# A gated recurrence followed by a maxout layer: the weights are requested through another engine's queue, the filling products are spread differently, and the written order of the whole program is replaced

## The chip, the cores and the metric

The program runs on one NeuronCore of one Trainium2 chip. The metric is device time in microseconds (us) of one execution. The kernel before takes 151.06 us, the median of 3 runs (150.87 to 151.34). A profiled execution has a span of its own: the time from its first to its last instruction.

In the text TensorE is PE (its weight loads PEld), VectorE is DVE, ScalarE is ACT, GpSimd is POOL and SyncE is SP. SP and ACT can both request transfers from memory (DMAs); each has a queue of its own.

## The reference, cut to what matters

```
def _attn_ref(q, k, v, alpha):            # 4 batches, 8 heads, 768 steps, 48 wide, float32
    state = zeros((B, H, D, D))
    for t in range(S):
        state = alpha[:, :, t, :, None] * state + einsum('bhd,bhe->bhde', k[:, :, t], v[:, :, t])
        y[:, :, t] = einsum('bhd,bhde->bhe', q[:, :, t], state)

def _moe_ref(x, w1, w2, w3, w_out):       # x: 3072 x 384 (y with its heads side by side)
    h = maximum(maximum(x @ w1, x @ w2), x @ w3)      # w1, w2, w3: 384 x 768
    return h @ w_out                                  # w_out: 768 x 384
```

## The kernel before, in words

The work is cut into 24 units: unit u is batch u % 4 and the chunk u // 4 of 128 time steps, with all 8 heads. Units 2n and 2n+1 share the loads number n of alpha, q, k and v (tiles `an`, `qn`, `kn`, `vn`). The loads 0 to 3 are asked for in halves, one unit each (192 KB in runs of 192 bytes: 8 heads by 48 floats). A load is named by the letter, n, and 0 or 8 for the first or second unit of the pair: "v 0 0" is v of unit 0, "q 1 8" is q of unit 3.

For each unit there is a chain of named steps. `ln` (ACT) takes the logarithm of alpha; `cums` (PE) sums it along time with a triangular matrix; `ep` and `en` (ACT) are its exponentials; `q~` and `k~` (DVE or POOL) scale q and k; `v` (ACT or POOL) scales v. `turn` (PE) transposes q~ and k~, `qkT` (DVE or ACT) copies them out of PSUM, `scores` (PE) multiplies them, `LA` (DVE) masks them, `outs` (PE) makes y, `xb` (ACT or DVE) casts it, `x turn` (PE) and `xT` (DVE or ACT) turn it into the layout of the layer. The state that is handed to the next chunk goes through `totals`, `e`, `G`, `sums`, `U` and `Z`.

The layer is computed from differences: max(x w1, x w2, x w3) = x w1 + max(0, x (w2 - w1), x (w3 - w1)). `grow` (PE, line 642) multiplies xT by one of the two differences, `relu` (ACT) and `max` (DVE) take the maximum, and `shrink` (PE, line 678) multiplies by w_out. What is left of x w1 is folded ahead: x (w1 w_out), made once by `w1 turn`, `w1T` and `fold` (line 383) and copied by `w1o`. In the names, "grow 1 0 0" is unit 1, the first half of the columns (the last but one digit 0), w2 - w1 (the last digit 0; 1 is w3 - w1).

All weights come in as float32, each matrix in two parts: "weights g p" (line 327) with g = 0 for w1, 1 for w2, 2 for w3, 3 for w_out; part 0 is the first 256 of 768 columns (384 KB), part 1 the other 512 (768 KB). Their tiles are `ws0` to `ws3`. `cast 0 p` (ACT, line 333) makes w1 half precision, `sub g p` (DVE or POOL, line 341) makes w2 - w1 and w3 - w1 (tile `wd`), and `cast 3 p` casts w_out. The first half of the columns of a `grow` needs both parts of `sub`; the second half needs part 1 alone.

The order of everything is written out by hand. The function builds a list of steps (`plan.step`), each with its engines to choose from. `ORDER` is the sequence of all steps over all engines, `PICK` chooses another engine than the first for some steps, `BANKS` gives each product its PSUM bank. `Plan.issue` runs down `ORDER`; every engine then executes its own steps strictly in that sequence. Loads, weights, cross transposes and stores begin in the order of the plan.

A DMA waits, on the engine that requests it, for the landing of the DMA eight places before it in the order of the plan, since they share eight semaphores. All steps that stand behind it on that engine wait along.

`zeros` are products of a cleared tile with itself (`Z1_0`, line 586), whose result nobody reads. They stand in PE's sequence between its early steps: 27 of them, the first behind `k~ 1`'s landing in its tile (`WARM = (1, 1, 27)`: unit, side, number).

Of the kernel before, what the change touches and what calls it, by code (L numbers as in the profile page):

```python
# [15 lines left out]

CDEC = 0.92
SIG = 128.0

NBANKS = 8  # L20
LEAD = (2.0, 4.0, 6.5, 5.0)
WCUTS = (0, 256, 768)
HALF_LOADS = 4
WARM = (1, 1, 27)
SINGLE, LAST = 4, 2
PAIRS = 10
CASTING = ()
# [5 lines left out]


ORDER = (
# [44 lines left out]
)  # L80
BANKS = (
# [9 lines left out]
)  # L91
PICK = {
# [8 lines left out]
}  # L101


TRANSFERS = ("load", "weights", "cross", "store")
BEHIND = mybir.DependencyInfo(mybir.DependencyClass.NoSync, mybir.DependencyReason.DATA)
HARD, HARD_LOAD, HARD_LATE, LATE_FROM = 0.5, 1.8, 1.5, 3


# [4 lines left out]
def weight_options(share, cast):  # L113
    if cast:
        return [("POOL", 0.6 + 0.4 * share, 0, 3.7 * share, 0.2)]
    return [("SP", HARD, 0, 3.25 * share + 0.1, 0.6)]


def cross_options(work):
# [55 lines left out]
def kernel(  # L175
# [12 lines left out]
    nc = tc.nc  # L188
# [85 lines left out]
        return at  # L274

    hq, ht = rotate(QKS, MORE[0]), rotate(QKTS, MORE[1])
    for t in las:
        nc.vector.memset(t[:, :, D:], 0.0)
    for t in qks[:QKS]:
        nc.vector.memset(t[:, :, :, D:], 0.0)  # L280
    for zz in Zs:
        for t in zz:
            nc.vector.memset(t, 0.0)

    plan = Plan()
    place, live = {}, {}
# [291 lines left out]
                      out=xT, in_=live[xk]),  # L578
                  reads=[xk], writes=[("xT", cb % NX, b)])

    def warm(u, w, count):
        zero = Zs[1][0].rearrange("p a b -> p (a b)")

        def zeros(e):
            live["wm"] = bank(("wm", 0), [P, DM], FP32)
            nc.tensor.matmul(live["wm"], zero[:, :P], zero, start=True, stop=True)  # L586

        for i in range(count):
            plan.step(f"zeros {i}", [("PE", 0.163)], 90.0, zeros,
                      banks=[("wm", 0)] if i == 0 else [],  # L590
                      reads=([("qk", hq[u], w)] if u >= 0 else []) if i == 0 else [("wm", 0)],
                      writes=[("wm", 0)] if i in (0, count - 1) else [])

    def state(u):
# [122 lines left out]
    for n in range(NG):  # L717
# [6 lines left out]
        for u in range(n * UB, (n + 1) * UB):  # L724
            prep(u)
            if u >= PAIRS and u % UB == 0:
                continue
            if u == WARM[0]:
                warm(*WARM)
            for v_ in (u - 1, u) if u >= PAIRS else (u,):  # L730
                output(v_)
        while due and due[0][-1] // UB + 4 <= n:
# [37 lines left out]
```

## Time and profile before

| | before |
|---|---|
| time, median of 3 | 151.06 us |
| the profiled execution's own time | 150.59 us |
| its span | 148.8 us |
| PE busy | 133.9 us (90%) |
| DVE busy | 106.9 us (72%) |
| ACT busy | 90.5 us (61%) |
| POOL busy | 52.5 us (35%) |
| mean granted PE clock | 0.977 |
| moved by DMA | 31.07 MB, mean 209 GB/s |

Two things help in reading it. PE's share is an average: PE has idle stretches in the first 26 us and none that matter behind them. And the 1.8 us between the span and the execution's own time lie outside the instructions.

### The profile page before, as it was taken

The page shows a single profiled execution, that of the slowest core. Times are in us where ns is not written, and L with a number is a line of the kernel's source. Part 1 is how long each engine was busy: PE and PEld are TensorE (multiplying, and loading weights), DVE is VectorE, ACT ScalarE, POOL GpSimd, SP SyncE. Part 2 cuts the span into 40 slices and gives each one's busy share as a digit, 9 for nine tenths or more (in the row PEclk, how much of TensorE's full clock was granted, in tenths as well). Part 3 has the DMA queues.
Part 4 walks back from the last instruction along what each step waited for, and adds up shares of the span by engine and source line. Part 5 has one row for each costly group of instructions (what it writes and reads, how often), then busy time and mean ns, then how long its engine had stood idle before and what let it go on. Part 6 is the DMA issues. An engine that isn't in the chain of part 4 may idle for free.

```text
span 148.8 us, 4162 instructions
## 1 busy us (share of the span) xinstructions
PE 133.9 (90%) x1683; PEld 104.6 (70%) x1683; DVE 106.9 (72%) x186; ACT 90.5 (61%) x184; POOL 52.5 (35%) x75
## 2 busy tenths in 40 slices
PE   0575297999999999999999999999999999999991
PEld 0233266968787886888787797787878877689781
DVE  7239318487998898979697779998578878584140
ACT  3531976948667587797746686745475844554331
POOL 0050041202523414840597709448029290170000
PEclk9999659999999999999999999999999999999999
DMA  5999999999999999999999999899998999704322
GB/s 115 205 225 322 202 341 269 283 267 173 223 208 219 237 220 210 248 184 250 266 266 263 185 197 250 163 215 269 177 232 160 243 325 189 147 4 131 109 82 79
DMA packets 116131, 31.07 MB, mean 209 GB/s; under 512 B 109712, under 2 KB 114960, under 8 KB 116112
## 3 DMA queue, kind: packets, MB, share of 16 engines
q1 hardware_dynamic: 83888, 21.17, 69.7%
q10 hardware_dynamic: 32224, 9.64, 28.7%
q8 instruction: 13, 0.21, 0.6%
q14 instruction: 6, 0.05, 0.1%
HBM read 23.69 MB, written 4.72 MB: 191 GB/s over the span
## 4 chain that ended last, share of the span: by engine, by line
PE 85%; SPq 5%; DMA 4%; ACT 2%; DVE 2%; issue 0%; ACTq 0%
PE psum L642 33%; PE psum L678 24%; PE psum L499 5%; PE psum L483 4%; SPq L308 4%; DMA vn<-in_v_dram 4%; PE psum L545 3%; PE psum L572 3%; PE psum L442 3%; PE psum L542 2%; PE psum L604 2%; PE psum L383 2%; PE psum L586 2%; PE psum L412 1%; DVE wd L341 1%; ACT w1h L333 1%
## 5 line engine op out<-in xcount | busy, mean ns | idle before, releaser
L642 PE MATMUL psum<-xT,wd 128*128 128x256 f16 (+1 forms) x540 | 54.4, 251 | 0.9 <-DVE wd L341 0.9
L642 PEld LDWEIGHTS <-wd 128*128 128x128 f16 x540 | 42.9, 98 | 6.9 <-DVE wd L341 1.7
L658 DVE TENSOR_TENSOR hT<-psum,hT 128x512 f16<-128x512 f32 (+1 forms) x39 | 24.3, 644 | 10.3 <-PE psum L642 4.7
L504 DVE TENSOR_TENSOR LA<-psum,c 128x1024 f16<-128x1024 f32 x24 | 28.6, 1219 | 3.1 <-PE psum L499 2.5
L653 ACT ACTIVATE hT<-psum 128x512 f16<-128x512 f32 (+1 forms) x39 | 21.5, 570 | 14.6 <-PE psum L642 13.6
L678 PE MATMUL psum<-wo,hT 128*128 128x384 f16 (+1 forms) x150 | 27.7, 320 | 0.0
L617 POOL TENSOR_TENSOR Z<-U,G 48x192 f16<-48x192 f32 x29 | 16.4, 572 | 12.5 <-DVE U L611 11.4
L678 PEld LDWEIGHTS <-hT 128*128 128x128 f16 x150 | 14.5, 98 | 8.9
L454 POOL TENSOR_TENSOR qk<-qn,ep 128x384 f16<-128x384 f32 x11 | 10.9, 998 | 15.1 <-ACT ep L447 13.3
L678 PE MATMUL psum<-w1o,xT 128*128 128x384 f16 (+1 forms) x75 | 15.8, 319 | 0.0
L450 ACT ACTIVATE en<-psum 128x384 f32<-128x384 f32 x24 | 11.9, 495 | 4.3 <-PE psum L442 3.8
L402 ACT ACTIVATE la<-an 128x384 f16<-128x384 f32 (+1 forms) x16 | 10.8, 689 | 5.7 <-DMA an<-in_alpha_dram 5.7
L454 POOL TENSOR_TENSOR qk<-kn,en 128x384 f16<-128x384 f32 x8 | 8.3, 1042 | 16.6 <-ACT en L450 12.7
L556 ACT ACTIVATE xb<-psum,c 128x384 f16<-128x384 f32 x16 | 9.1, 582 | 8.0 <-PE psum L545 5.8
L447 ACT ACTIVATE ep<-psum 128x384 f32<-128x384 f32 x24 | 11.7, 496 | 2.6 <-DVE qk L454 0.9
L693 ACT COPY ob<-psum 128x384 f32<-128x384 f32 (+1 forms) x18 | 8.3, 468 | 7.8 <-PE psum L678 5.1
L442 PE MATMUL psum<-la,c 128*128 128x384 f16 x24 | 7.8, 347 | 5.6 <-ACT la L402 5.5
L461 ACT ACTIVATE v<-vn,c 128x384 f16<-128x384 f32 x14 | 8.3, 614 | 6.2 <-DMA vn<-in_v_dram 6.2
L545 PE MATMUL psum<-v,LA 128*128 128x48 f16 x192 | 11.1, 186 | 0.0
L611 DVE TENSOR_TENSOR U<-psum,Z 128x384 f32<-128x384 f32 x16 | 8.5, 551 | 3.1 <-PE psum L604 2.5
L545 PEld LDWEIGHTS <-LA 128*128 128x128 f16 x192 | 9.8, 98 | 0.6 <-issue 0.2
L464 POOL TENSOR_SCALAR v<-vn,c 128x384 f16<-128x384 f32 x10 | 6.3, 635 | 9.4 <-DMA vn<-in_v_dram 9.0
(61 smaller groups left out, 189.6 us busy)
## 6 DMA issues: line engine op xcount, KB each, us to landing
out_dram<-ob ACTq DMA_DIRECT2D x20, 192.0 KB, 3.3
an<-in_alpha_dram SPq DMA_DIRECT2D x7, 384.0 KB, 6.6
ws<-in_moe_w_dram SPq DMA_DIRECT2D x3, 768.0 KB, 6.1
kn<-in_k_dram SPq DMA_DIRECT2D x5, 384.0 KB, 6.5
vn<-in_v_dram ACTq DMA_DIRECT2D x5, 384.0 KB, 6.6
an<-in_alpha_dram SPq DMA_DIRECT2D x8, 192.0 KB, 4.0
kn<-in_k_dram SPq DMA_DIRECT2D x8, 192.0 KB, 4.4
qn<-in_q_dram ACTq DMA_DIRECT2D x4, 384.0 KB, 5.3
```

The costliest lines, as they stand in the source:

```text
L402: lambda e, lo=lo * H, hi=hi * H: nc.scalar.activation(out=la[:, lo:hi, :D], in_=an[:, lo:hi, :], func=AFT.Ln, scale=1.0 / CDEC),
L442: nc.tensor.matmul(live[Lk], tri, la[:, hs, :D], start=True, stop=True)
L447: lambda e: nc.scalar.activation(out=ep, in_=live[Lk], func=AFT.Exp),
L450: lambda e: nc.scalar.activation(out=en, in_=live[Lk], func=AFT.Exp, scale=-1.0),
L454: lambda e, w=w, x=x, d=d: engines[e].tensor_mul(qk[:, w, :, :D], ld[x][n % LOADED][:, hs], d),
L504: lambda e: nc.vector.tensor_mul(LA.rearrange("p a b t -> p (a b) t"), live[Ak].rearrange("p a (b t) -> p (a b) t", t=P), maskA.unsqueeze( ...
L545: nc.tensor.matmul(yp[:, 2 * j + p, :], LA[:, p, j, :], v16[:, 2 * j + p, :], start=(cb == 0), stop=True, skip_group_check=True)
L617: lambda e, rows=rows, cols=cols: engines[e].tensor_mul(Zn[rows, :, cols], (Us[u % 3] if cb else live[pk])[rows, :, cols], G[rows, i * NP: ...
L642: nc.tensor.matmul(live[gk][:, jj, :], wd[:, kt, g, j * P:(j + 1) * P], xT[:, kt, :], start=(kt == 0), stop=(kt == NFT - 1))
L653: lambda e, h=h, gk=gk: nc.scalar.activation(out=h, in_=live[gk], func=AFT.Relu),
L658: lambda e, h=h, gk=gk: nc.vector.tensor_max(h, live[gk], h),
L678: nc.tensor.matmul(live[ok][:, cols], a[:, i * P:(i + 1) * P], w[:, cols], start=(kt == 0), stop=(kt == nk - 1))
```

## The change

Four edits go together.

1. A weight request may now go through ACT (a second choice in `weight_options`), and the new `PICK` takes it for all eight (among its first rows: 32, 34, 36 to 40 and 42). None is left on SP.
2. The zero products: 46 instead of 27, without the dependence on `k~ 1`. The tile that they multiply is cleared first of all on DVE.
3. `ORDER`, `BANKS` and `PICK` are new from the first to the last row. The numbers of the steps shift by the 19 added zeros.
4. With it some steps change engines: `sub 1 1` and `sub 2 0` go from DVE to POOL; `qkT` moves towards ACT (7 instead of 4), `ob` towards DVE (12 instead of 7), stores towards SP (10 instead of 4), loads towards ACT (21 instead of 15).

```
-WARM = (1, 1, 27)
+WARM = 46
 ORDER = (
-    4, 8, 9, 5, 6, 0, 10, 12, 34, 7, 32, 1, 11, 2, 123, 65, 127, 82, 84, 128, 129, 83, 64, 131,
...
+    6, 4, 0, 10, 8, 20, 5, 1, 9, 3, 2, 32, 64, 65, 34, 142, 78, 68, 121, 92, 146, 120, 66, 80,
...
-    return [("SP", HARD, 0, 3.25 * share + 0.1, 0.6)]
+    return [("SP", HARD, 0, 3.25 * share + 0.1, 0.6), ("ACT", 0.45, 0, 3.25 * share)]
...
+    nc.vector.memset(Zs[1][0], 0.0)
     for t in las:
         nc.vector.memset(t[:, :, D:], 0.0)
     for t in qks[:QKS]:
         nc.vector.memset(t[:, :, :, D:], 0.0)
-    for zz in Zs:
-        for t in zz:
-            nc.vector.memset(t, 0.0)
+    for t in Zs[0] + Zs[1][1:]:
+        nc.vector.memset(t, 0.0)
...
-    def warm(u, w, count):
+    def warm(count):
...
-                      reads=([("qk", hq[u], w)] if u >= 0 else []) if i == 0 else [("wm", 0)],
+                      reads=[("wm", 0)] if i else [],
...
-            if u == WARM[0]:
-                warm(*WARM)
+            if u == 0:
+                warm(WARM)
```

Three places show what the new tables do. The first is the start of SP's sequence before: loads (`an`, `kn`, `qn`, `vn`) and weights (`ws0` is w1, `ws1` is w2) stand in one line.

```order
L308 DMA an1_67<-in_alpha_dram 128x8x48
L327 DMA ws0_150<-in_moe_w1_dram 128x3x512
L308 DMA vn0_78<-in_v_dram 128x8x48
L327 DMA ws0_150<-in_moe_w1_dram 128x3x256
L308 DMA kn0_74<-in_k_dram 128x8x48
L308 DMA vn1_79<-in_v_dram 128x8x48
L308 DMA qn0_70<-in_q_dram 128x8x48
L327 DMA ws1_151<-in_moe_w2_dram 128x3x256
L327 DMA ws1_151<-in_moe_w2_dram 128x3x512
```

Now the weights stand in ACT's sequence, here from the cast of w1 on (line 335) to the request of w3's larger part (`ws2`). Between them are `ep` (449), `v` (463), the copies `w1T` (374), `qkT` (492) and `xb` (558).

```order
L335 CAST w1h_148<-ws0_150 128x3x512
L449 ACTIVATE ep0_85<-psum_177 128x384
L335 CAST w1h_148<-ws0_150 128x3x256
L463 ACTIVATE v0_100<-vn0_78,c32_62 128x384
L329 DMA ws1_151<-in_moe_w2_dram 128x3x512
L374 COPY w1T_149<-psum_177 128x768
L463 ACTIVATE v1_101<-vn0_78,c32_62 128x384
L329 DMA ws1_151<-in_moe_w2_dram 128x3x256
L492 COPY qkT2_109<-psum_177 128x1024
L329 DMA ws3_153<-in_moe_w_out_dram 128x2x384
L374 COPY w1T_149<-psum_177 128x768
L558 ACTIVATE xb1_116<-psum_177,c32_62 128x384
```

What moved: a weight is no longer behind other transfers in SP's line, but behind whatever ACT has to do ahead of it. The two parts of w1 are requested earlier in the same sequence, around the first `ln` steps.

The second place is the difference w2 - w1 (`wd` from `ws1` and `w1h`) that the first `grow` needs. Its larger part stood in DVE's sequence before, behind an `LA` (504) and an `xT` (577):

```order
L558 TENSOR_SCALAR xb2_117<-psum_177,c32_62 128x384
L504 TENSOR_TENSOR LA0_112<-psum_177,c16_61 128x1024
L577 COPY xT0_120<-psum_177 128x3x128
L341 TENSOR_TENSOR wd_154<-ws1_151,w1h_148 128x3x512
L577 COPY xT0_120<-psum_177 128x3x128
```

Now both of its parts stand in POOL's, behind the early `q~` and `k~` steps (456) and one `v` (466), and the smaller part of w3 - w1 follows:

```order
L456 TENSOR_TENSOR qk2_93<-kn1_75,en2_90 128x8x48
L456 TENSOR_TENSOR qk2_93<-qn1_71,ep2_87 128x8x48
L456 TENSOR_TENSOR qk0_91<-qn0_70,ep0_85 128x8x48
L466 TENSOR_SCALAR v2_102<-vn1_79,c32_62 128x384
L343 TENSOR_TENSOR wd_154<-ws1_151,w1h_148 128x3x512
L343 TENSOR_TENSOR wd_154<-ws1_151,w1h_148 128x3x256
L343 TENSOR_TENSOR wd_154<-ws2_152,w1h_148 128x3x256
```

What moved: DVE has one such step left (`sub 2 1`), POOL three, in a row.

The third place is the start of PE's sequence. Now one zero product (line 588) stands ahead of the first `cums` (444), which needs the first load of alpha, and two behind it:

```order
L588 LDWEIGHTS Z1_0_137
L588 MATMUL psum_177<-Z1_0_137 128x384
L444 LDWEIGHTS c16_61
L444 MATMUL psum_177<-la0_82,c16_61 128x384
L588 LDWEIGHTS Z1_0_137
L588 MATMUL psum_177<-Z1_0_137 128x384
L588 LDWEIGHTS Z1_0_137
L588 MATMUL psum_177<-Z1_0_137 128x384
```

What moved: before, two `cums` came first and nine zeros behind them. In all, 43 of the 46 zeros now stand ahead of the first `grow` (23 of 27 before), and the last three among the first five.

More of the change, by code (lines that the diff above doesn't have):

```diff
@@ L18 @@
 SIG = 128.0
+TRANSFERS = ("load", "weights", "cross", "store")
+BEHIND = mybir.DependencyInfo(mybir.DependencyClass.NoSync, mybir.DependencyReason.DATA)
 NBANKS = 8
@@ L35 @@
 ORDER = (
[44 rows of a table removed]
[45 rows of a table added]
 )
 BANKS = (
[9 rows of a table removed]
[9 rows of a table added]
 )
 PICK = {
[8 rows of a table removed]
-}
-TRANSFERS = ("load", "weights", "cross", "store")
-BEHIND = mybir.DependencyInfo(mybir.DependencyClass.NoSync, mybir.DependencyReason.DATA)
[9 rows of a table added]
+}
 HARD, HARD_LOAD, HARD_LATE, LATE_FROM = 0.5, 1.8, 1.5, 3
```

122 rows, old and new, of tables (BANKS, ORDER, PICK) are left out of this document.

## The prediction

> **What bounds the kernel now.** I read the slices of the page first (PE at 9 tenths from the eighth slice on), then busy time by stretches of my own choosing, then the chain that ended last. The stretches are cut where the granted clock changes, at the first `grow` (25.69 us) and at the first `shrink` (37.39 us). The columns are length, busy time of PE, PEld, DVE, ACT and POOL with counts, granted clock, DMA share, GB/s.
>
> ```profile
> 9.09:12.50 3.41, 2.41 (x30) 1.43 (x28) 1.19 (x3) 0.23 (x1) 0.99 (x1) 1.00 0.99 279
> 12.50:15.92 3.42, 0.82 (x15) 0.32 (x9) 2.55 (x3) 1.41 (x4) 0.00 (x0) 1.00 1.17 270
> 15.92:19.33 3.41, 1.62 (x12) 1.29 (x13) 1.12 (x2) 3.09 (x5) 0.00 (x0) 0.50 0.87 228
> 19.33:22.75 3.42, 3.42 (x39) 2.26 (x37) 1.09 (x2) 2.55 (x4) 1.64 (x1) 0.50 1.10 352
> 22.75:25.69 2.94, 2.05 (x37) 1.53 (x36) 2.77 (x3) 2.25 (x5) 0.58 (x1) 1.00 1.16 273
> 25.69:37.39 11.70, 11.67 (x170) 9.56 (x171) 7.78 (x10) 8.85 (x19) 2.18 (x3) 1.00 0.96 237
> 37.39:145.78 108.39, 108.36 (x1383) 86.62 (x1381) 85.14 (x143) 67.99 (x142) 45.93 (x65) 1.00 1.02 201
> 145.78:148.80 3.02, 0.00 (x0) 0.00 (x0) 0.36 (x1) 0.00 (x0) 0.00 (x0) 1.00 0.29 98
> ```
>
> From 25.69 to 145.78 us PE is idle for 0.06 us. The rest of the span is a start of 25.7 us, in which PE waits or multiplies zeros, and an end of 3.0 us for the last copy and store. So the program is PE's work plus the time until PE has enough of it. Two stretches of the start run at half the clock (0.50), after a stretch in which PE was busy for 0.82 of 3.42 us.
>
> The chain (start, us, what) says what the start waits for.
>
> ```profile
> 16.29 1.37 ACT w1h L333
> ...
> 17.71 0.82 PE psum L366 x6
> ...
> 23.97 1.68 DVE wd L341
> ...
> 25.69 1.18 PE psum L642 x18
> 26.87 0.16 PE psum L586
> 27.03 0.17 PE psum L572 x3
> ...
> 37.39 1.49 PE psum L678 x9
> ```
>
> w1's larger part is cast at 16.29 us; then PE works on the first three units at half the clock; DVE comes to `sub 1 1` (line 341) at 23.97 us; `grow` (642) begins. A zero product (586) costs 0.16 us at full clock, an `x turn` (572) 0.17.
>
> **The frame of the sum.** Up to `shrink 0 0 0` both orders hold the same 42 steps on PE, zeros aside, and behind it the same steps too, with no zeros. So the span after is (start of the first `shrink`) + 108.4 + 3.0 us, as long as PE is not kept waiting later. I take that wait as zero: the closest hand-overs of the long part stand alike in both orders (`x turn 14`, one copy `xT 14`, then `grow` with 0.55 us of PE work between; `scores 20`, `LA 20`, `outs 20` with 1.46), and PE lost 0.03 us there before. What must be found is when the first `grow` begins, 25.69 us before.
>
> **w1 arrives earlier.** The rows are DMA issues (out<-in, queue, count, size, median us from issue to landing), then requests on SP in order of time.
>
> ```profile
> out_dram<-ob ACTq DMA_DIRECT2D x20, 192.0 KB, 3.3
> ...
> ws<-in_moe_w_dram SPq DMA_DIRECT2D x3, 768.0 KB, 6.1
> ...
> an<-in_alpha_dram SPq DMA_DIRECT2D x8, 192.0 KB, 4.0
> ...
> c<-const ACTq DMA_DIRECT2D x1, 96.5 KB, 2.4
> ```
>
> ```profile
> 0.74 1.07 SPq L308 DMA_DIRECT2D an<-in_alpha_dram  x2
> ...
> 6.70 0.76 SPq L308 DMA_DIRECT2D an<-in_alpha_dram  x1
> 7.51 1.10 SPq L327 DMA_DIRECT2D ws<-in_moe_w_dram  x1
> ...
> 15.34 1.25 SPq L327 DMA_DIRECT2D ws<-in_moe_w_dram  x2
> ```
>
> The eighth load was requested at 6.70 us, so it landed near 10.7 (4.0 later); the first near 4.7: 0.86 us apart. After, SP's first loads are the same kind. w1's smaller part waits on ACT for the fourth of them (it holds that semaphore), 7.3 us; two `ln` of 0.5 us follow, and the larger part goes out at about 8.3 us. Alone it would need 2.4 us (the small constant, nearly all latency) plus its bytes: 768 KB at the 352 GB/s of the best stretch is 2.2 us, so 12.9 us. In a line with loads it took 6.1, so 14.4. A 192 KB store on ACT's queue lands in 3.3 us while loads on SP's take 4.0 and more, so a large request on the second queue is not held up by the first; I take 13.4 us. The page "DMA: Bandwidth & Descriptors" of the Trainium skill (Queues, rings and completion order) says that each DMA engine takes turns between the queues by packet, which would favour 2 KB weight rows over 192-byte load rows; no row here has the two kinds side by side.
>
> **From w1 to the first `grow`.** ACT is the line that everything passes. Before, from the cast to `xb 0`, it was busy for 3.09 + 2.55 + 2.25 = 7.9 us and idle for 1.9 of 9.8. ACT's own rows of before give the prices:
>
> ```profile
> 14.51 0.61 ACT L461 ACTIVATE v<-vn,c 128x384 f16<-128x384 f32 x1 [5.19 <-DMA vn<-in_v_dram]
> 15.03 0.51 ACT L402 ACTIVATE la<-an 128x384 f16<-128x384 f32 x1
> ...
> 41.66 0.48 ACT L693 COPY ob<-psum 128x384 f32<-128x384 f32 x1
> 41.67 0.42 ACTq L308 DMA_DIRECT2D qn<-in_q_dram  x1
> ```
>
> After, the stretch holds one more `v` (0.61) and two `ln` (0.5 each, a little overlapped) for one short `e`: about 9.2 us. The five weight requests in it I cost at nothing: the last two rows show a request that runs beside the copy ahead of it. If that cover is gone (ACT idle and waiting there), each costs 0.42 us, 2.1 in all. With ACT's idle time a little under what it was (1.8 us; PE is warm this time, since the zeros leave it no long gap), `xb 0` ends at 13.4 + 9.2 + 1.8 = 24.4 us, and the first `grow` can begin at 24.6.
>
> It needs `sub 1 1` too.
>
> ```profile
> 20.02 1.64 POOL L341 TENSOR_TENSOR wd<-ws,w1h 128x768 f16<-128x768 f32 x1 [9.30 <-DMA ws<-in_moe_w_dram]
> ...
> 23.89 1.75 DVE L341 TENSOR_TENSOR wd<-ws,w1h 128x1536 f16<-128x1536 f32 x1
> ```
>
> POOL takes 1.64 us for half as many elements as DVE does in 1.75, so `sub 1 1` costs about 3.3 us there instead. w2's larger part is requested when ACT starts `v 0`: a cast (1.37), an `ep` (much like an `ln`) and a cast of half the size are 2.6 us, so 16.0 us, about as before (16.1, the second of the two at 15.34). It lands 4.9 us later (2.4 + 2.2 + some sharing; bounds 4.6 and 6.1), 20.9 us. `sub 1 1` ends at 24.2, `sub 1 0` at 25.8. So the slower engine is hidden: both lines meet at 24.6 us. The third `grow` is the first that needs `sub 1 0`, at 25.6: 0.2 us of waiting.
>
> **The sum.** First `grow` 24.6 instead of 25.69: -1.1. Behind it `x turn 0` is done already (-0.17) and one zero product fewer stands in the way (-0.16). New: 0.2 at the third `grow`, and 0.3 at `scores 3`, whose `qkT 3` moves to ACT behind four `relu` and a `w1o`. Together -0.9 us. `fold` needs w_out, which follows w2 in ACT's queue: the 1.5 MB from w2's smaller part to w_out's larger are 4.4 us at 352 GB/s, so 25.3 us, with some sharing 26, and cast by 28; five `grow`, three zeros and what stands between end at 27.9. Met, without a margin. w3 comes last; its parts are subtracted by 33 us, and the order asks for them at 33 and 34. The 16 zeros that are idle fill in the start cost nothing, as PE waits there anyway; nothing of the 46 stands behind the first `shrink`.
>
> So the first `shrink` begins at 36.5 us, the span is 147.9 us and the execution 149.7 (the span and 1.8 us around it, as in the profiled 150.59). The median of three is 0.5 above the profiled run, so I forecast 150.2 us.
>
> Bounds: w1 at 12.9 and no new waits give -1.9 us; w1 at 14.4 gives +0.1, and uncovered requests add up to 2.1. This case's own range is 149.0 to 150.7.
>
> **Rivals.**
>
> *The loads hold the weights up: slower.* ACT's line is strict. w2's request stands behind `v 0`, which needs the tenth load on SP. At 0.86 us each that is 12.4 us, plus the 3.3 us in which w1 (1.15 MB at 352 GB/s) takes the memory: 15.7, and it is needed at 16.0. In the trace of before ACT stood still for 5.19 us in front of just such a `v`. The third `grow` can begin 4.9 us (landing) and 3 x 1.64 us (POOL) after the request; from a request at 16.9 us on that is 26.7, no earlier than before (25.69 and two `grow` of 0.5), and the gain is gone. If w1 takes its 6.1 us instead of 3.3, the tenth load comes at 18.5 and the `grow` 1.6 us later than before: 152.7 us. For it: a faster w1 means slower loads, for they share one memory path, at a DMA share near 1. Against: only ten loads are asked for. Chance 0.24.
>
> *Nothing is gained: the queues share one service.* Loads asked for before w1 are served before it; w1 lands at 14.5 us and the whole start moves by 1.1 us, onto the old place: 151.3 us. For it: the share of the DMA engines is 0.9 to 1.2 throughout. The same page of the Trainium skill (Issuing engines are not separate DMA queues) speaks for it: requests from several engines interleave on the same 16 DMA engines, and only issue time is saved. By that sentence the whole gain would be gone. Chance 0.14.
>
> *The clock is lost again.* "From the first microsecond" is one zero product; the next follow the first `cums`, after 7 us. A stretch with PE busy for 24% was followed by half the clock, one with 71% was not. From 14.8 us on PE has 24 zeros (3.8 us) and some 4.5 us of products for 9.8 us, 85%, so I expect the clock to hold. If loads leave a gap and it falls for 6.8 us, as before, PE does 3.4 us of that work instead of some 5.8: 2.4 later, of which 1.0 falls into idle time: 151.6. Chance 0.08.
>
> *A wait in the long part.* Every sequence is new; one bank or one load that is late there costs PE directly. 0.5 to 2 us: 150.7 to 152.2. Chance 0.06.
>
> **How the numbers follow.** Forecast 0.48, rivals 0.24, 0.14, 0.08, 0.06. The time is that of the forecast, 150.2. The range 149.0 to 152.6 takes in its lower bound, the case of no gain, the lost clock, the late wait and most of the case with held-up weights. A measurement of this kernel can tell about 0.3% (0.45 us) from no change. Faster by more: nearly all of the forecast and a little of the late wait, 0.49. Within it: the case of no gain and a part of the clock's, 0.16. Slower: 0.35.
>
> **What would show it.** Right: cast of w1 near 13.4 us, first `grow` near 24.6, first `shrink` near 36.5, then PE busy for 108.4 us. Wrong: ACT idle ahead of `v 0` for a DMA for over 1 us; a granted clock of 0.50 anywhere from 15 to 25 us; idle time of PE behind the first `shrink`.

## The result, and the profile after

| | before | after |
|---|---|---|
| time, median of 4 | 151.2 us | 157.0 us (155.56 to 158.31) |
| ratio | | 1.038, 95% interval 1.0315 to 1.0447 |
| profiled execution, its span | 150.59, 148.8 us | 157.59, 155.8 us |
| first `grow`, first `shrink` by the chain | 25.69, 37.39 us | 29.60, 40.70 us |
| from there to the end | 111.4 us | 115.1 us |
| mean granted PE clock | 0.977 | 0.967 |

The change makes the kernel slower by 3.8%; 150.2 us was forecast. Of the 7.0 us of span, 3.3 are lost up to the first `shrink` and 3.7 behind it.

PE's slices of the page after show two holes, each with a fall of the clock beside it (a slice is 3.9 us):

```profile
PE   1095799999999999999499999999999999999992
...
PEclk9999559999999999999969999999999999999999
```

The same stretches as in the prediction, cut at after's own places (length, busy time of PE, PEld, DVE, ACT and POOL with counts, granted clock, DMA share, GB/s):

```profile
9.09:12.50 3.41, 3.41 (x19) 1.72 (x18) 0.00 (x0) 2.02 (x5) 0.65 (x1) 1.00 1.10 340
12.50:15.60 3.10, 1.34 (x8) 0.59 (x6) 0.74 (x2) 0.64 (x1) 0.46 (x2) 1.00 0.83 184
15.60:19.30 3.70, 2.67 (x24) 1.97 (x24) 0.98 (x2) 3.66 (x6) 3.05 (x3) 0.54 1.07 249
19.30:23.10 3.80, 3.80 (x30) 2.55 (x25) 1.22 (x1) 1.01 (x1) 1.71 (x2) 0.55 1.15 313
...
40.70:73.98 33.28, 33.28 (x451) 26.70 (x449) 29.65 (x56) 22.93 (x47) 12.97 (x22) 1.00 1.15 219
73.98:76.27 2.29, 0.04 (x1) 0.01 (x1) 2.29 (x2) 0.52 (x2) 1.81 (x2) 1.00 1.25 245
76.27:82.50 6.23, 6.23 (x52) 3.77 (x53) 3.87 (x6) 2.94 (x6) 2.65 (x4) 0.73 0.85 203
82.50:152.80 70.30, 70.26 (x882) 56.56 (x880) 52.20 (x88) 37.27 (x78) 27.75 (x41) 1.00 0.88 166
```

DVE does nothing at all from 9.09 to 12.50 us; before, units 1 and 2 were scaled by 10.7. PE is then busy at half the clock. In the middle PE stands still for 2.25 us, while DVE is busy without a pause, and the next 6.23 us run at a mean clock of 0.73. That is worth up to another 1.7 us (an estimate, 0.27 x 6.23); what is left of the 3.7 us beside the stop is 1.45. One of the four executions had a granted clock of 1.00 throughout and still took 155.56 us, 2.0 less than the profiled one. By that the clock is some 2 us of the profiled execution's loss, and most of the loss is something else.

The chain that ended last, in the start:

```profile
14.96 1.48 ACT w1h L335
...
19.55 0.76 PE psum L588 x2
...
21.16 1.28 PE psum L588 x4
...
25.38 0.92 PE psum L588 x5
...
29.60 1.51 PE psum L644 x27
...
40.70 1.46 PE psum L680 x9
```

Zero products (line 588) are links of it. The next rows are the loads beside w1 (DMA issues between 6.6 and 8.5 us, with the median time to landing), the spread of the three of k, and the first scaling on DVE that waited for them:

```profile
ws<-in_moe_w_dram ACTq DMA_DIRECT2D x1, 768.0 KB, 7.2
kn<-in_k_dram SPq DMA_DIRECT2D x3, 192.0 KB, 7.9
...
vn<-in_v_dram SPq DMA_DIRECT2D x1, 192.0 KB, 7.7
```

```profile
DMA to landing us min/median/max: 3.5/7.9/8.1
```

```profile
14.86 1.03 DVE L456 TENSOR_TENSOR qk<-kn,en 128x384 f16<-128x384 f32 x2 [10.66 <-DMA kn<-in_k_dram]
```

And before, the two loads of v that were asked for beside w1 in the one queue, and the first scaling on DVE:

```profile
vn<-in_v_dram SPq DMA_DIRECT2D x2, 192.0 KB, 6.0
```

```profile
7.02 0.56 DVE L454 TENSOR_TENSOR qk<-kn,en 128x384 f16<-128x384 f32 x1 [2.81 <-ACT en L450]
```

The first load of k, asked for at 5.9 us, ahead of w1, took 3.5 us; the loads beside w1 take nearly 8. Before, v and k beside w1 took 5.8 to 6.6 us, so loads beside w1 were slow in one queue too, and two queues added 1 to 2 us. The larger part of w1 takes 7.2 us, where it took 6.1; only its smaller part came sooner after its request (5.1 us instead of 6.4). The first `k~` on DVE begins at 14.86 us, 7.02 before. Two things make it late: the new order asks for k of unit 0 as the eighth load (before, two of the first four loads were k), and w1 stands beside it on the other queue.

And ACT's own line in the start:

```profile
21.20 1.01 ACT L492 COPY qkT<-psum 128x1024 f16<-128x1024 f16 x1 [1.94 <-PE psum L485]
...
24.93 0.80 ACT L374 COPY w1T<-psum 128x768 f16<-128x768 f16 x1 [2.72 <-PE psum L368]
24.94 0.38 ACTq L329 DMA_DIRECT2D ws<-in_moe_w_out_dram  x1
```

ACT waits for PE twice, 4.7 us together, and the request of w_out's larger part, which stands behind the second wait, goes out at 24.94 us (17.16 before).

### The profile page after: what moved, and what is told of

It is laid out like the page before. It is cut to its first block, busy times and chain, and to the rows that moved or that the text cites. A ratio compares the mean times of both kernels' runs of the same rounds, so it can differ in the third digit from the quotient of the medians.

```text
span 155.8 us, 4195 instructions
## 1 busy us (share of the span) xinstructions
PE 139.8 (90%) x1702; PEld 107.6 (69%) x1702; DVE 105.3 (68%) x187; ACT 88.2 (57%) x176; POOL 58.1 (37%) x82
## 4 chain that ended last, share of the span: by engine, by line
PE 81%; DMA 7%; DVE 4%; ACT 3%; SPq 1%; issue 1%; ACTq 0%
PE psum L644 29%; PE psum L680 23%; PE psum L501 5%; PE psum L485 5%; DMA ws<-in_moe_w_dram 5%; PE psum L547 3%; PE psum L574 2%; DMA qn<-in_q_dram 2%; PE psum L588 2%; PE psum L544 2%; PE psum L606 2%; DVE ws L456 2%; PE psum L444 2%; SPq L310 1%; PE psum L414 1%; PE psum L385 1%
## 5 line engine op out<-in xcount | busy, mean ns | idle before, releaser
L644 PE MATMUL psum<-xT,wd 128*128 128x256 f16 (+1 forms) x540 | 53.7, 251 | 0.0
L680 PE MATMUL psum<-wo,hT 128*128 128x384 f16 (+1 forms) x150 | 28.5, 328 | 0.0
L619 POOL TENSOR_TENSOR Z<-U,G 48x192 f16<-48x192 f32 x31 | 15.6, 508 | 29.3 <-DVE U L613 24.1
L456 POOL TENSOR_TENSOR qk<-qn,ep 128x384 f16<-128x384 f32 x12 | 11.8, 996 | 12.2 <-ACT ep L449 12.0
L588 PE MATMUL psum<-Z 128*128 128x384 f16 x46 | 13.2, 410 | 1.1 <-DVE Z L279 1.1
L466 POOL TENSOR_SCALAR v<-vn,c 128x384 f16<-128x384 f32 x12 | 7.0, 585 | 14.9 <-DMA vn<-in_v_dram 14.5
L456 DVE TENSOR_TENSOR qk<-kn,en 128x384 f16<-128x384 f32 x8 | 4.7, 598 | 10.7 <-DMA kn<-in_k_dram 10.7
L456 POOL TENSOR_TENSOR qk<-kn,en 128x384 f16<-128x384 f32 x9 | 9.2, 1026 | 6.1 <-ACT en L452 3.3
L588 PEld LDWEIGHTS <-Z 128*128 128x128 f16 x46 | 4.8, 116 | 8.8 <-issue 6.7
L695 ACT COPY ob<-psum 128x384 f32<-128x384 f32 (+1 forms) x13 | 6.1, 467 | 8.1 <-PE psum L680 8.1
```

The lines of the kernel that those rows point to most:

```text
L456: lambda e, w=w, x=x, d=d: engines[e].tensor_mul(qk[:, w, :, :D], ld[x][n % LOADED][:, hs], d),
L619: lambda e, rows=rows, cols=cols: engines[e].tensor_mul(Zn[rows, :, cols], (Us[u % 3] if cb else live[pk])[rows, :, cols], G[rows, i * NP: ...
L644: nc.tensor.matmul(live[gk][:, jj, :], wd[:, kt, g, j * P:(j + 1) * P], xT[:, kt, :], start=(kt == 0), stop=(kt == NFT - 1))
L680: nc.tensor.matmul(live[ok][:, cols], a[:, i * P:(i + 1) * P], w[:, cols], start=(kt == 0), stop=(kt == nk - 1))
```

## The experiments

Ratios are to the kernel before, run beside each experiment on the same chip. "First" times of the experiments are starts in PE's timeline; by it before has its first `grow` at 25.69 and its first `shrink` at 37.25, after at 29.43 and 40.53.

### The stop at 74 us: three scalings on DVE, then one

```
 PICK = {
+    402: 1, 403: 1, 410: 1,        # q~ 12, k~ 12, q~ 13: DVE instead of POOL
```

> The changed kernel with k~ 12, q~ 13 and q~ 12 on DVE instead of POOL, nothing else. Theory (k~ 11 on DVE took 3.56 instead of 0.55 us because POOL worked without a pause beside it): k~ 11 ends by 74 us instead of 76.2, PE's gap of 2.3 us at 74 us is gone, and the half clock behind it as well; the time is 153 to 155. Rival (the load of k that landed at 72.83 us was late): the gap stays at 2 us or more and the time at 156.5 to 157.5.

153.75 us (153.41 to 154.99), ratio 1.0215 (1.0149 to 1.028), against 1.038. The step that PE waited for is `k~ 11`, the first of the two in DVE's row. The timeline of after around it, and the first of the two by itself (min, median and max in ns):

```profile
70.98 1.96 POOL L456 TENSOR_TENSOR ws<-qn,ep 128x384 f16<-128x384 f32 x2
71.46 1.28 DVE L660 TENSOR_TENSOR hT<-psum,hT 128x512 f16<-128x512 f32 x2
...
72.65 4.03 DVE L456 TENSOR_TENSOR ws<-kn,en 128x384 f16<-128x384 f32 x2
72.90 0.99 POOL L456 TENSOR_TENSOR qk<-kn,en 128x384 f16<-128x384 f32 x1
...
73.86 1.93 POOL L456 TENSOR_TENSOR qk<-qn,ep 128x384 f16<-128x384 f32 x2
...
76.27 0.34 PE L485 MATMUL psum<-c,ws 128*128 128x128 f16 x3 [2.25 <-DVE ws L456]
```

```profile
L456 DVE TENSOR_TENSOR ws<-kn,en x1: 3560/3560/3560, 72.7 to 72.7; 128x384 f16<-128x384 f32 x1
```

With the three steps on DVE:

```profile
69.55 1.95 POOL L455 TENSOR_TENSOR ws<-qn,ep 128x384 f16<-128x384 f32 x2
...
71.22 1.16 DVE L455 TENSOR_TENSOR ws<-kn,en 128x384 f16<-128x384 f32 x2
```

```profile
L455 DVE TENSOR_TENSOR ws<-kn,en x1: 693/693/693, 71.2 to 71.2; 128x384 f16<-128x384 f32 x1
```

`k~ 11` took 3.56 us after and 0.69 here. PE's stop is gone, and no half clock follows in the profiled execution. Four other runs below leave these three steps on POOL, and in each of them `k~ 11` takes 3.56 to 3.57 us and PE stands still for 2.2. The load of k that landed at 72.83 us was for POOL's `k~ 12`, not for this.

```
+    402: 1,                        # q~ 12 alone
```

> The changed kernel with q~ 12 alone on DVE; POOL has k~ 12 and q~ 13 left beside k~ 11. If POOL holds DVE off for as long as it works without a pause: k~ 11 lasts 2.5 to 2.7 us (3.56 with three), PE's gap shrinks from 2.3 to 1.2 to 1.5 us. If it is one operation of POOL that holds DVE off, whatever follows: 3.4 to 3.6 still, or 0.9 to 1.4.

```profile
71.95 3.08 DVE L455 TENSOR_TENSOR ws<-kn,en 128x384 f16<-128x384 f32 x2
...
72.20 1.00 POOL L455 TENSOR_TENSOR qk<-kn,en 128x384 f16<-128x384 f32 x1
73.15 0.99 POOL L455 TENSOR_TENSOR qk<-qn,ep 128x384 f16<-128x384 f32 x1
...
74.62 0.56 PE L484 MATMUL psum<-c,ws 128*128 128x128 f16 x7 [1.30 <-DVE ws L455]
```

```profile
L455 DVE TENSOR_TENSOR ws<-kn,en x1: 2614/2614/2614, 72.0 to 72.0; 128x384 f16<-128x384 f32 x1
```

The one execution of it took 155.21 us. `k~ 11` took 2.61 us and PE waited 1.3 us, as the first line expected. In all three runs `k~ 11` ends 0.41 or 0.42 us after POOL's last operation without a pause (75.79, 74.14 and 71.50 us): it does not start before POOL pauses. The page "SBUF — State Buffer" of the Trainium skill (Who interferes with whom, and its Summary: rules for kernel authors) says that a DVE operation with two inputs in SBUF and a GpSimd operation that reads SBUF exclude each other, and that the second to issue waits until the first finishes. The runs agree with the exclusion, but show a wait over as many operations as POOL has in a row. They also agree that one SBUF input does not contend: the two `max` (line 660, one input in PSUM) beside POOL's first two scalings took 0.68 us as elsewhere.

### Queue or order of the loads

```
 PICK = {
-    32: 1, 34: 1, 36: 1, 37: 1, 38: 1, 39: 1, 40: 1, 42: 1,      # after: all eight weights on SP again
```

> The changed kernel with its eight weight requests back on SP's queue, in the same written order. Theory (weights on a queue of their own pass the loads asked for before them, and the three units start late for it): the k load that took 8.1 us takes 3.5 to 5, the first k~ on DVE begins by 11.5 us instead of 14.86, the first shrink at 37.5 to 39 instead of 40.7; the time is 153.5 to 155.5. Rival (the new order of the loads is to blame, not the queue): the first k~ stays behind 14 us, the first shrink at 40 or later, the time 156.5 to 157.5.

159.34 us (157.07 to 160.15), ratio 1.048 (1.039 to 1.058): no faster than with the weights on ACT (1.038, 1.0315 to 1.0447), so neither text was right. In its profiled execution (159.56 us) the k loads take 3.8 to 4.0 us again and the first `k~` begins at 10.27 us, as the theory had it. But w1's larger part, now asked for behind eleven loads at 11.5 us, lands at 16.8. What the loads gain w1 loses. So the new order is slow by itself, without the second queue.

```
-    6, 4, 0, 10, 8, 20, 5, 1, 9, 3, 2, 32,
+    4, 8, 5, 9, 0, 1, 6, 10, 2, 3, 20, 32,      # after, with alpha and k of units 0 to 2 first
```

> The changed kernel with only its first eleven loads in another order: alpha and k of the first three units ahead of q, v and the early alpha of unit 5. The weights stay on ACT. If the order of the loads is to blame: the first k~ begins by 9 us and the first shrink comes at 37.5 or before, the time is 153 to 154. If it is the queue of the weights: k comes early, but q and v of the first units still land at 14.5 us or later, and the first shrink at 39 to 40.7; the time is 155 to 157.

157.08 us, ratio 1.041 (1.036 to 1.046): no gain, and at the upper end of what was expected if the queue is to blame. The first `k~` begins at 9.30 us, but the q loads beside w1 now take 7.2 to 7.7 us and land at 13.6 and 15.0. The first `grow` comes at 26.37 us at a full clock, and then PE waits in the folds for the cast of w_out:

```profile
31.54 1.79 PE L381 MATMUL psum<-wo,w1T 128*128 128x384 f16 x10 [1.48 <-ACT wo L331]
```

So the first `shrink` is at 39.97.

```
-    return [("SP", HARD, 0, 3.25 * share + 0.1, 0.6)]
+    return [("SP", HARD, 0, 3.25 * share + 0.1, 0.6), ("ACT", 0.45, 0, 3.25 * share)]
...
+    32: 1, 34: 1, 36: 1, 37: 1, 38: 1, 39: 1, 40: 1, 42: 1,      # before, all weights on ACT
```

> The kernel before, its order, banks and zeros as they are, with the eight weight requests on ACT's queue. If a second queue for the weights makes the loads late: loads that are under way beside w1 take 6 us and more, the first shrink moves from 37.4 to 38.4 or later, the time is 152.2 to 154. If the queue costs nothing: 150.8 to 151.6. If the earlier weights help, as the change meant: below 150.7.

156.06 us (155.58 to 156.5), ratio 1.035 (1.030 to 1.039), far beyond what was expected. This one edit, with the old order, banks and zeros, costs nearly what the whole change costs. The rows are DMA issues between 2.7 and 5.7 us, and the long wait:

```profile
ws<-in_moe_w_dram ACTq DMA_DIRECT2D x1, 768.0 KB, 5.2
...
qn<-in_q_dram SPq DMA_DIRECT2D x2, 192.0 KB, 6.7
...
an<-in_alpha_dram SPq DMA_DIRECT2D x1, 192.0 KB, 7.3
```

```profile
23.25 0.56 DVE L453 TENSOR_TENSOR qk<-qn,ep 128x384 f16<-128x384 f32 x1 [3.07 <-DMA qn<-in_q_dram]
...
23.86 0.61 PE L482 MATMUL psum<-c,qk 128*128 128x128 f16 x4 [4.65 <-DVE qk L453]
```

w1's larger part, asked for at 4.0 us, lands at 9.2, over 4 us earlier than before, and yet the first `grow` is 5 us later, at 30.67: q of unit 0 lands only near 23.2, behind the weights that passed it, and everything waits for that. Behind the first `shrink` nothing is lost (108.52 us of PE, as before), so it is not the same loss as that of the change, of which more than half lies there.

Together the four cases are: old order with the weights on SP 1, old order on ACT 1.035, new order on ACT 1.038, new order on SP 1.048. The queue costs 3.5% in the old order and nothing in the new one; the order costs 4.8% with the weights on SP. Each of the two is enough for most of the loss, and the losses do not add up.

```
+    32: 1, 34: 1,      # before, w1 alone on ACT
```

> The kernel before with only w1's two requests on ACT's queue; w2, w_out and w3 stay on SP. With all eight on ACT the first grow came at 30.67 us, and q of unit 0, asked for at 13.5 us beside w2 and w_out, landed at 23.2 us. If the flood of the later weights is what costs: w1 lands near 9 to 12 us, q of unit 0 by 19, first grow at 26 us or before, the time 150 to 152. If w1 ahead of the loads is enough to cost it: k and q loads of units 1 and 2 take 6 us and more, first grow at 27.5 or later, the time 153 to 155.

155.04 us (153.01 to 155.83), ratio 1.019 (1.009 to 1.029). Four of the loads beside w1 take 7.0 to 8.4 us, w1 lands at 10.7, and the first `grow` is at 26.97 us, between the two expectations. w1 ahead of the loads is enough to lose, and the later weights add to it. In both runs w1 is asked for some 3.4 us earlier than before (near 4.1 instead of 7.51) as well as on another queue; w1 asked for as early on SP was not tried, so the two are not told apart.

### Clock and zero products

In the trace of before the first nine zero products begin at 6.22 us, ahead of every `k~` (the first is at 7.02). Their dependence on `k~ 1` orders the plan and holds nothing up on the chip.

```
-            nc.tensor.matmul(live["wm"], zero[:, :P], zero, start=True, stop=True)
+            for _ in range({16: 16}.get(i, 1)):        # after: 15 more ahead of w1 turn 2
+                nc.tensor.matmul(live["wm"], zero[:, :P], zero, start=True, stop=True)
```

> The changed kernel with 15 more zero products ahead of the first w1 turn, where PE stood idle from 13.8 to 16.5 us. Clock theory: 1.00 from 15 to 25 us in every execution, first grow at 26 to 27 instead of 29.4, first shrink at 38.7 to 39.2, the time 154.5 to 156 (the stop at 74 us stays). Rival (the zeros themselves are on PE's path): first grow at 29 or later, time 157 or more.

156.34 us (155.13 to 158.38), ratio 1.028 (1.022 to 1.034). In the profiled execution the clock is 1.00 throughout the start, the first `grow` at 26.19 and the first `shrink` at 38.75 us, as the clock theory had it, and the time is 0.3 us above what it expected; the stop in the middle stays.

```
+            if i in (32, 36, 13, ..., 11, 1):        # after: 26 zeros behind w1 turn 2 left out
+                return
```

> The changed kernel without 26 of its zero products: those behind the first w1 turn, the last one kept. Nothing that is used is left out, since nobody reads these products. If the zeros at half the clock stand on PE's path: first grow at 27 to 28.5, the time 155 to 156. If they are filler in PE's waiting: first grow within 0.5 us of 29.4 at the same clock. If they keep the clock up: half the clock lasts longer than 7.5 us, the time 157.5 or more.

155.7 us (154.44 to 158.18), ratio 1.023 (1.015 to 1.031). The clock now stays low from 17.5 to 31 us,

```profile
17.50:27.60 10.10, 7.90 (x86) 6.00 (x87) 5.02 (x6) 6.40 (x12) 5.32 (x4) 0.50 1.07 302
```

and yet it gets faster. From the first `w1 turn` to the first `grow` it is 11.87 us, against 12.94 after (16.49 to 29.43) and 10.47 with a full clock and all zeros (15.39 to 25.86 with the three scalings). So zeros hold the clock up and stand on the path at the same time: without them the clock is low for nearly twice as long (13.5 us instead of 7.5) and PE is still 1.1 us sooner through.

```
-            nc.tensor.matmul(live["wm"], zero[:, :P], zero, start=True, stop=True)
+            for _ in range({20: 26}.get(i, 1)):        # before: 25 more ahead of w1 turn 2
+                nc.tensor.matmul(live["wm"], zero[:, :P], zero, start=True, stop=True)
```

> The kernel before with 25 more zero products at one place: ahead of the first w1 turn, where PE stood idle from 13.3 to 17.7 us. If the gap is what costs the clock (0.50 from 15.9 to 22.8 us): the clock stays at 1.00, the first grow comes at 24 to 25.3 instead of 25.69, the time is 149.2 to 150.3. If the loads set the start whatever the clock is: clock full, first grow at 25.5 to 26, time within 0.4 of the kernel before. If the clock falls for another reason: 0.50 again, no change.

153.0 us against 151.83 for the kernel before, ratio 1.0067 (1.0029 to 1.0104). The profiled execution is the fastest of the twelve, 151.39 us. In it the clock stays at 1.00 and the first `grow` still comes at 25.37, 0.3 us earlier. What ended last there:

```profile
22.23 1.75 DVE L341 TENSOR_TENSOR wd<-ws,w1h 128x1536 f16<-128x1536 f32 x1
...
22.77 1.66 POOL L464 TENSOR_SCALAR v<-vn,c 128x384 f16<-128x384 f32 x1 [1.24 <-DMA vn<-in_v_dram]
...
24.48 0.36 PE L545 MATMUL psum<-v,LA 128*128 128x48 f16 x8 [2.33 <-POOL v L464]
```

`v 0` waits for its load, and then for DVE: 1.66 us instead of 0.58, the same exclusion with the roles exchanged. So the half clock of before cost next to nothing: at a full clock a load and this exclusion end last, 0.3 us earlier. Why the run is even slower was not settled.

### What is left of the loss

The three scalings on DVE and the 15 zeros of above together:

> The changed kernel with both repairs: k~ 12, q~ 13 and q~ 12 on DVE, and 15 more zero products ahead of the first w1 turn. If the stop at 74 us and the lost clock are the whole loss: 150.7 to 151.7, level with before. If the late transfers of the start cost as well, as the first shrink at 38.7 us with a full clock says (1.3 to 1.5 us late): 152.5 to 154, clock at 1.00 throughout, first shrink at 38.5 to 39.

153.62 us (153.19 to 153.83), ratio 1.017 (1.011 to 1.023), the granted clock 1.00 in all four executions, first `shrink` at 38.91. So the stop and the clock are not all: about 2.4 us are left. (The 15 zeros are too many by 1 us here: they end at 16.50, while w1's cast was done at 15.6.)

```
-    ... 133, 36, 153, 40, 13, 14,
+    ... 133, 36, 40, 42, 153, 13, 14,      # w_out's two requests (40, 42) moved up, with the three scalings on DVE
```

> The changed kernel with k~ 12, q~ 13 and q~ 12 on DVE (153.75 us) and, besides, both requests of w_out moved up in ACT's line, right behind the request of w2's smaller part. Without this its larger part went out at 21.75 us, behind a copy of ACT that waits for PE, landed at 28.42, and PE waited 1.0 us in and behind the folds. If that place in ACT's line is what keeps the start late at a full clock: w_out lands by 26.5, the wait ahead of the folds is gone, first shrink at 37.3 to 38.2 instead of 38.72, the time 152.4 to 153.3. If the memory path is full there anyway: w_out lands earlier, but k and q of unit 3 later than 26 us, first shrink at 38.6 or later, the time 153.5 or more.

152.14 us (150.7 to 153.04), ratio 1.0054 (1.0013 to 1.0096), against 1.0215 with the three scalings alone. ACT's requests of w_out's larger part and the folds, first without, then with the edit:

```profile
21.75 0.38 ACTq L328 DMA_DIRECT2D ws<-in_moe_w_out_dram  x1
...
29.97 1.79 PE L384 MATMUL psum<-wo,w1T 128*128 128x384 f16 x10 [0.42 <-ACT wo L334]
```

```profile
18.58 0.50 ACTq L324 DMA_DIRECT2D ws<-in_moe_w_out_dram  x1
...
29.68 2.11 PE L380 MATMUL psum<-wo,w1T 128*128 128x384 f16 x12
```

The request goes out 3.2 us earlier, but takes 9.5 instead of 6.7 us and lands only 0.35 us earlier, at 28.07, not by 26.5 as expected. PE's waits for w_out and `w1o` (0.42 and 0.56 us) are gone all the same, in part because PE comes to the folds 0.6 us later (w1 landed later in this execution), and the first `shrink` comes at 38.26 instead of 38.72. The rest of the gain lies behind it: 108.58 us of PE instead of 110.24, since waits of 0.9, 0.5 and 0.2 us for a cross transpose, an `ob` and a scaling are gone. That these go because of w_out's place was not shown. But this kernel has the new order, all its zeros and all eight weights on ACT, and it is 0.5% behind the kernel before, where the change was 3.8%: nearly all of the loss goes with five places in the tables, three scalings on POOL and two requests behind ACT's waits.

```
+            if i in (32, 36, 13, ..., 11, 1):        # the 26 late zeros out, with the three scalings on DVE
+                return
```

> The changed kernel with k~ 12, q~ 13 and q~ 12 on DVE and without the 26 zero products behind the first w1 turn. If the zeros are the rest of the loss: first shrink at 37.5 or before, the time 151 to 152.3. If w_out sets the first shrink and the zeros only fill: first grow up to 1.5 us earlier than 25.86 at a full clock, but first shrink at 38.4 to 39.2 and the time 153 to 154.5. If the clock falls without the zeros: half the clock for over 8 us, first shrink at 39.5 or later, the time 153.5 to 155.

155.15 us (152.58 to 155.95). Three executions ran at a mean clock of 0.94 (154.92 to 155.95), one at 1.00 (152.58, where the full-clock ones with the zeros took 153.4 and 153.8). The third line held in the main (its time was to be at most 155): without these zeros the clock mostly falls.

```
-    110, 36, 37, 3, 42,
+    110, 3, 36, 37, 42,      # before: v of unit 0 ahead of w2; gap filled; zeros 2, 13, 17 and 26 left out
```

> The kernel before with the gap filled as in the run before, v of unit 0 asked for ahead of w2, and the four zero products behind the first grow left out. With the gap filled, PE waited 2.3 us for v 0 on POOL, which took 1.66 instead of 0.58 us beside a difference on DVE. If that collision and that load set the start: v 0 takes 0.6 us again, first grow at 24 to 24.8, first shrink at 36 to 36.8, the time 0.3 to 1.2 us below the kernel before. If w_out's landing sets the first shrink whatever comes ahead of it: fold at 30.3 or later, first shrink within 0.4 us of 37.1, the time within 0.5 us of the kernel before.

151.22 us against 151.23, ratio 1.0016 (0.9957 to 1.0075): no change. That fits the line that w_out's landing sets the start, but only the time is used here, so the landing was not shown. None of the versions that were run beats the kernel before.

## Why the prediction was wrong, step by step

The span was to be 147.9 us and was 155.8. Of the 7.9 us, 4.2 lie ahead of the first `shrink` (40.70 instead of 36.5 us) and 3.7 behind it. By the chain the start splits into w1, 1.5 us late, the line from w1 to the first `grow`, 3.5 longer, and the rest, 0.8 shorter.

**The frame: no wait in the long part. Failed.** The work behind the first `shrink` is the same, 108.5 us, once nothing stands in its way (108.58 with w_out earlier). But the term taken as zero was 3.7 us: 2.25 us of stop and some 1.45 us that go with the half clock behind it. I compared the hand-overs in the two orders, where a step has one price. The price of `k~ 11` depends on what POOL does beside it: 0.55 us or 3.56. The trace of before had a hint of it: `k~` on DVE took from 0.54 to 1.23 us there. The rival "a wait in the long part" was put at 0.5 to 2 us and 0.06. Its time was too short by half, and its chance much too low for a wholly new order.

**w1 lands at 13.4 us: off by 0.5 to 1.5.** 14.94 in the profiled execution, 13.85 to 14.45 in the others that were read. It was asked for 0.6 us earlier than in the sum (7.74 instead of 8.3 us) and took 7.2 us instead of 5.1. Taking 2.2 us for the bytes assumed that the loads beside it yield; both sides slowed down instead. The page "DMA: Bandwidth & Descriptors" of the Trainium skill (Issuing engines are not separate DMA queues) had it right, that several queues interleave on the same engines. Its turns by packet between queues agree with loads beside w1 that go from 5.8 to 6.6 us in one queue to 7.7 to 8.1 on two, but w1's larger part did not land sooner after its request for it. The rows of before had the two kinds side by side after all, within one queue.

**The line from w1 to the first `grow`, 11.2 us: the step that failed most in the start.** It was 14.5 us. I took ACT's own work with 1.8 us of idle time. Its waits for PE alone were 4.7 us. All of the three units' PE work came behind w1, since the first scaling in DVE's line, `k~ 0`, needed a load that landed at 14.8 us; before, two units were half done by then. At a full clock the line is 12.0 us (13.87 to 25.86 with the three scalings), so 0.8 of the miss is there at a full clock too and 2.5 go with the clock of this execution.

**"The 16 zeros that are idle fill cost nothing, as PE waits there anyway": wrong.** Once PE is late, they are on its path.

**The clock holds: wrong.** The argument, PE busy for 85% from 14.8 us on, overlooked the 2.65 us ahead of it. Of that rival (0.08, 151.6 us) the trigger was right, a gap that loads leave, and its price nearly so: 2.4 us of delay, 1.4 of them left at the first `shrink`. The runs show 2.5 us on the line and 1.8 at the first `shrink` (40.53, against 38.75 with the gap filled). Its chance was too low.

**Weight requests on ACT cost nothing: right as issue time, wrong as place.** A request took 0.4 us beside a copy. But it also inherits the waits ahead of it, and w_out, forecast for 26, landed at 30.78.

**The rival "the loads hold the weights up"** had the right quarrel and the wrong loser: w2's request went out at 16.07, as forecast (16.0). The loads were held up by the weights. "Queues share one service" was true of the transfers, but did not end in no change, since the loads that came late were the ones that were needed.

**Right:** POOL's two differences in 4.70 us (4.9), and two of the three signs of failure that were named, half the clock between 15 and 25 us and idle time behind the first `shrink`. The differences with w3 were to be ready by 33 us and were ready at 34.9 and 37.5; PE, late itself, did not wait for them.

## What to carry to other kernels

Here the DMA engines' share was 0.8 to 1.2 in every stretch of the start that is shown, in both kernels, and a second queue did not add to it: it changed who was late. Before moving requests, list what each engine needs first, and check that those bytes still come first. Price a two-input step of DVE with its neighbours on POOL in view, and when an order is new throughout, give "some step meets another" a chance well above that of a single edit.

## What the runs showed of the hardware

- DVE's scaling (two inputs in SBUF) waits for as long as POOL scales without a pause: 0.69, 2.61 and 3.56 us for none, two and three POOL operations that follow the one under way, the last in five runs alike. The other way round, POOL's `v` took 1.66 instead of 0.58 us beside a DVE difference.
- PE's first products run at half speed although the granted clock reads 1.00. These two rows are zeros at 8.21 us (two) and 22.92 us (three); a product starts 0.32 us after the last in the first and 0.16 in the second:

```profile
8.21 0.84 PE L588 MATMUL psum<-Z 128*128 128x384 f16 x2
...
22.92 0.65 PE L588 MATMUL psum<-Z 128*128 128x384 f16 x3
```

  Full speed came at 12.5 us after and by 9.4 before, 4.6 and 3.8 us after continuous work began, so the one zero product in the first microsecond, which before does not have, did not shorten it. The page "TensorE: Matmul & The Clock Gate" of the Trainium skill (Part 1) has this as its default state, half the clock until some 3.4 us of sustained work; the runs agree in kind, with 3.8 and 4.6 us, but for the granted clock that is shown.
- Half the clock followed idle times of PE of 2.25 us (the stop), 2.65 and 2.8, and one of 1.5 us with little work behind it, but not 1.6, 2.0, 2.3 and 2.6 us. So the length of one gap does not tell it. After 3.0 us, in before with w1 alone on ACT, the granted clock stays at 1.00, yet three zero products at 16.43 us take 1.17 us together, where three at full speed took 0.65: a granted clock of 1.00 does not prove full speed. The same page (HAM oscillation) warns of gaps over about 3.4 us. Here shorter ones were enough, and the same program had the fall in one execution and, by the granted clock, not in another (mean 0.967 and 1.000).
